# An attention block with a mixer MLP in one kernel: the last 64 rows of a product contracted beside row maxima, three maxima inside a product instead of four, and q loaded in step 2

## The chip, the core and the metric

The kernel runs on one core of one Trainium2 chip. The metric is the device time of one execution in microseconds (us): before the change the median of three runs is 1121.79 us (1120.84 to 1122.47). One further execution was taken by the profiler, and the trace is that execution's.

## The reference

Everything is float32 with S = 2048 tokens, D = 448 columns, H = 16 heads of 28 columns and an MLP of F = 1792. LN is layer norm without weights.

```python
mod = (silu(c) @ w_mod).reshape(1, 6, 1, 448)          # sa, ca, ga, sb, cb, gb
h = LN(x) * (1 + ca) + sa
q, k, v = split(h @ wqkv)                              # 16 heads of 28 columns
p = softmax(q @ k.T * 28 ** -0.5)                      # 2048 x 2048 for each head
x = x + ga * ((p @ v) @ wo)
h = LN(x) * (1 + cb) + sb
x = x + gb * (gelu(LN(h) @ w1 + b1) @ w2 + b2)
```

The softmax subtracts the maximum of each row of the scores before the exponential. The kernel has to find these row maxima before it can compute the exponentials, and most of what follows is about where it does so.

## The kernel before, in words

**Precision.** Matmuls read a rounded 32-bit form. To get float32 products, an operand is split into a rounded part `hi` and the residual `lo`, and a product is the sum of hi·hi, hi·lo and lo·hi.

**Stages.** Setup (0 to 29 us) computes the modulation of the first half and splits the weights. Stage 1 (29 to 168 us) computes q, k and v. Stage 2 (168 to 826 us) is the attention. Stage 3 (827 to 1121 us) is the MLP.

**Stage 1** runs over four blocks b of 512 tokens, and in each block over *tasks*, written (b,n) here. A task is one product with 448 contracted rows: q or k of four heads (a head group g) for 512 tokens (`qk_task`, L415), or v for 128 tokens (`v_task`, L450). In blocks 1 and 2 there are eleven tasks: q and k of the groups 1 and 2, q of group 3 (whose k is carried in spare columns of the others), four of v, and q and k of group 0 of the next block. Block 3 has eight, and the last has no maxima. 448 rows are three chunks of 128 and one of 64. `terms448` (L400) makes eleven matmuls of them, three for each full chunk and two for the last. In the last chunk x stands twice: rows 0 to 63 hold its hi part, rows 64 to 127 its residual (`split_chunk`, L280), and the weights' rows are doubled too, so that one matmul of 128 rows gives hi·hi and lo·hi together and a second gives hi·lo. `mm_acc` (L390) issues the eleven; at the middle it can call a *mid-product visit*, `emit_mid` (L715), which is set for the tasks (1,1), (1,3), (1,5), (1,7) and (2,8) only.

**Row maxima.** One maximum is a matmul (L476) that contracts the 28 columns of a head for 128 queries with 512 keys, and a reduction on VectorE (L481). The four heads of a group stand in partitions 0, 32, 64 and 96, the *row groups* 0 to 3 of TensorE; row groups 0 and 1 are called half 0, and 2 and 3 half 1. A unit (a head group g and a block qt of 512 queries) needs 64 such maxima: 4 heads, 4 tiles of queries, 4 chunks of keys. There are 16 units, so 1024 maxima. In stage 1 some are found in *pairs*: with the difference of two key chunks as operand, max(a, b) = b + relu(a − b), where ScalarE takes the relu (L489) and VectorE adds and reduces in one instruction (L493). Which units and query tiles may pair in stage 2 stands in `PAIR_ROWS` and `PAIR_AT` (L36, L37; there the relu is L641 and the reduction L648).

`emit_task` (L691) issues the maxima that follow a product: four in block 0 and five after it, a sixth in a tile of its own where `p1_n[1]` allows it, with one to three pairs (`p1_n[2]`). It takes the pairs from the front of their list, emits their difference matmuls, then two single maxima, then the second matmuls of the pairs, then the other singles. The results go through a ring of PSUM tiles (`ma`, `ma`, `m2`, `m2`, `m1` at most; in the profile `ma` and `m`), and the next matmul into a tile waits for VectorE to have read it. `p1_n` is set for each task at L837 and below.

**Stage 2** takes the 16 units one after the other, each in 16 *steps* of 128 keys (kt = 0 to 15), 256 steps in all; `clock[0]` is the step's number. A step has twelve score matmuls (L1297), six for each half, two exponentials on ScalarE (L1310) and the product with v of the step before (L1255). Beside them stand maxima of the units that come next, `n_max` of them: before step `RING` (119) four in even steps and three in odd ones (or two and the closing of a pair). `n0` of them go between the score matmuls of the first half and are sought in half 1 (`emit_single(1, ...)`); the others come at the end of the step and are sought in half 0. From `RING` on a step has one single maximum and `emit_pair` (L670): two maxima of one half in one two-bank tile, reduced together (L684); where no such couple is ready, it puts two single maxima one after the other into that tile. Steps 8 to 11 of the last four units (`is_wo`) hold the output product with `wo` and three maxima.

**What ends a unit's preparation.** When the last of a unit's 64 maxima is counted, `max_fin` reduces them, and two steps later they are written into spare rows of the unit's q tile by four DMAs (L525, L528). The q tile must have been loaded by then: `load_q` (L777, whose DMAs are at L770; `slot_b` in the profile) is asked for in step 6 of the unit before. When 64 maxima of a key chunk or of a query block are counted, the next head group's k or q for its maxima is loaded (`load_hi`, L508, `kh` and `qh` in the profile); `loaded` makes these available three steps later. All these DMAs are issued by SyncE, whose queue (SPq in the profile) works in program order: one that waits holds up those behind it. In it stand also, for the unit that has ended, the sums of the softmax (`den`, L998, step 1 of the next unit), their reciprocals to memory and back (L1006 and L1008, step 4, or step 2 in the last units), and the next group's operands (`load_k`). GpSimd multiplies by the reciprocals in step 10 (L1013), in step 7 of the last unit.

Of the kernel before, what the change touches and what calls it, by code (L numbers as in the profile page):

```python
# [16 lines left out]
ALU = mybir.AluOpType  # L17
# [5 lines left out]
D = 448  # L23
# [8 lines left out]
NTT = S // 128  # L32
P1RATE = 4
LAST_MAX = NKT - 4
RING = 119
PAIR_AT = (2, 2, 0, 2)  # L36
PAIR_ROWS = {(0, 2): 2, (0, 3): 3, (1, 0): 2, (1, 1): 2}  # L37
WO_MAX = 3
YTAGS = [f"{a}{i}" for a in ("kh", "qh") for i in range(4)]
EPS = 1e-5  # L40
# [4 lines left out]
def tile_adaln_block(ctx: ExitStack, tc: tile.TileContext, x, wqkv, wo, w1, b1, w2, b2, c, w_mod, out):  # L45
# [72 lines left out]
    def f(t):  # L118
        return t.bitcast(F32)
# [160 lines left out]
    def split_chunk(k, full, hi, lo, eng, hi_copy=None):  # L280
        if hi_copy:
            hi_copy(hi, full)
        if k < 3:
            eng.tensor_tensor(out=lo, in0=full, in1=f(hi), op=ALU.subtract)
        else:
            eng.tensor_tensor(out=hi[64:128], in0=full[64:128], in1=f(hi)[64:128], op=ALU.subtract)

    hT = {}

# [102 lines left out]
    def mm_acc(p, terms, mid=None):  # L392
        for i, (a, b) in enumerate(terms):
            if mid and i == len(terms) // 2:
                mid()
            pe.matmul(p, a, b, start=(i == 0), stop=(i == len(terms) - 1))  # L396

    def terms448(x_hi, x_lo, w_hi, w_lo):  # L400
# [13 lines left out]

    def qk_task(b, kind, g, begun=None):  # L415
        p, ts = begun or qk_terms(b, kind, g)
        if begun is None:
            mm_acc(p, ts, p1_n[3])
        emit_task(*p1_n[:3])
        if g == 0:  # L420
            tg = ("kh" if kind else "qh") + str(b)
            hi = sb.tile([128, 512], F32R, tag=tg, name=nm(tg), bufs=1)
            (kh_sb if kind else qh_sb)[(g, b)] = hi
        elif g == 1 and b < 2:

            hi = sbt("raw" if kind else "osb", [128, 512], F32R, bufs=3 if kind else 2)
            (kh_sb if kind else qh_sb)[(g, b)] = hi
        else:
            hi = sbt("hi", [128, 512], F32R, bufs=3)
        full = sbt("full", [128, 512], bufs=3)  # L430
        lo = sbt("lo", [128, 512], F32R, bufs=3)
        act.copy(full, p)

        def split():
            (act.copy if b else dve.tensor_copy)(hi, full)
            if kind == 1 and (g, b) == (0, 1):
                k_diff.append(sbt("raw", [128, 512], F32R, bufs=3))
                pool.tensor_tensor(out=k_diff[0], in0=f(hi), in1=f(kh_sb[(0, 0)]), op=ALU.subtract)
            pool.tensor_tensor(out=lo, in0=full, in1=f(hi), op=ALU.subtract)
            sl = slice(b * 512, (b + 1) * 512)  # L440
            for part, t in enumerate((hi, lo)):
                sp.dma_start(f(dscr[kind][part][g])[:, sl], f(t))

            if b < 3 or g == 0 or (kind, g) == (0, 1):
                put_spare()
            spare.append((kind, g, sl))

        return split

    def v_task(b, t, p):  # L450
        ts = slice(t * 128, (t + 1) * 128)
        hh, hl = hT[b]
        mm_acc(p[:, :D], terms448(
            lambda k: hh(k)[:, ts], lambda k: hl(k)[:, ts], lambda k: wv[0][:, k, :], lambda k: wv[1][:, k, :],
        ), p1_n[3] if phase1[0] else None)
        if phase1[0]:
            emit_task(*p1_n[:3])
        act.copy(v_sb[b][:, t, :, :DH], p[:, :D].rearrange("p (h d) -> p h d", d=DH))


# [2 lines left out]
    mxq = []  # L463
# [224 lines left out]
            emit_single(half, lambda: t[:, jj])  # L688


    def emit_task(n, sixth, n_pairs):  # L691
        if not n:
            return
        pairs = [pxq.pop(0) for _ in range(min(n_pairs, len(pxq)))]
        rests = [pair_diff(*m) for m in pairs]
        js = [m[3] for m in pairs]
        n_ops = n - len(pairs) + (sixth and len(pairs) > 0)
        singles = []
        for x in range(n_ops - len(pairs)):
            if mxq:  # L700

                free = [j for j in range(4) if j not in js] or range(4)
                fits = [y for y, m in enumerate(mxq[:16]) if m[:3] == mxq[0][:3] and m[4] == free[x % len(free)]]
                singles.append(mxq.pop(fits[0] if fits else 0))
        ops = [lambda ps, m=m: max_one(*m, ps) for m in singles]
        ops[2:2] = rests
        for x, op in enumerate(ops):
            op(ps_o if x + len(pairs) == 5 else ps_mx)
        for g, qt, cch, i, j in singles:
            count(g, qt, [cch])  # L710
        for g, qt, i, j in pairs:
            count(g, qt, [0, 1])


    def emit_mid():  # L715
        for j in range(4):
            fits = [x for x, m in enumerate(mxq[:16]) if m[4] == j]
            if fits:
                m = mxq.pop(fits[0])
                max_one(*m)  # L720
                count(*m[:2], [m[2]])

    p1_n = [0, False, 1, None]

    def finish_max(g, qt):
        if px_open and px_open[0][0][:2] == (g, qt):
# [86 lines left out]
    for b in range(NB):  # L813
# [12 lines left out]
        for n, (tb, kind, g) in enumerate(tasks):  # L826
            post = []
            ready, newq = newq, []
            if not more and n == len(tasks) - 2:

                mx_ring[:] = ["ma", "ma", "m2", "m2", "m1"]
            p1_n[0] = P1RATE if b < 1 else P1RATE + 1
            if not more and n == len(tasks) - 1:
                p1_n[0] = 0

            k = n - (6, 4, 4, 4)[b]
            p1_n[1] = not (more and (0 <= k < NC)) and not (b == 1 and n < 4)  # L837
            p1_n[2] = (3 if n > 4 else 1) if b == 3 else 2 if b == 2 and p1_n[1] else 1
            p1_n[3] = emit_mid if (b, n) in ((1, 1), (1, 3), (1, 5), (1, 7), (2, 8)) else None
            if kind < 2:  # L840
                fn = qk_task(tb, kind, g, firsts[n] if b == 0 and n < 3 else None)
                if g == 0:
                    fn()
                else:
                    post.append(fn)
                if kind == 1 and (g == 0 or (g == 1 and tb < 2)):
                    newq = [(g, qt, cch) for qt in range(tb + 1) for cch in range(tb + 1) if max(qt, cch) == tb]
            else:
                v_task(tb, g, ps_s())
            for item in ready:  # L850
                queue_max(*item)
            if b == 0 and 2 <= n < 6:
                prep_w(2, n - 2, act.copy, dve)
            if more:
                k = n - (6, 4, 4, 4)[b]

                if b == 0 and n in (0, 1, 3, 4):
                    x = 2 * n if n < 2 else 2 * n - 2
                    for fn in stages[x : x + 2]:
                        fn(xs_next)  # L860
                if b and n < 4:
                    stages[n](xs_next)
                if 0 <= k < NC:
                    post.append(h_chunk(b + 1, xs_next, k))
                if later and 7 <= n < 11:
                    later[n - 7](None)
            if n == (4 if b else 6):
                v_init(b)
            if b == 0 and n == 6:
                mod_load(0)  # L870
                mod_load(1)
            if b == 1 and n == 8:
                put_last_rows()
            if b == 2 and n == 5:
                sp.dma_start(b1_col, b1.rearrange("(k p) -> p k", p=128))
            if b == 1:
                if n < 2:
                    mod_mm(n)
                    mod_load(2 + n)
                elif n in (2, 3):  # L880
                    mod_mm(n)
                    if n == 3:
                        mod_fin()
            if not more:
                if n == 0:
                    load_q(0)
                    load_q(1)
                if n == 4:
                    load_k(0, 0)
                if n == 5:  # L890
                    act.activation(cols[:, 0:1], zero_col, AF.Exp)
                if n == 2:
                    put_ones(0)
            tick_late()
            if not more and n == 5:
                for ch in range(1, 4):
                    load_k(0, ch)
            for fn in post:
                fn()
# [331 lines left out]
    def is_wo(s_):  # L1231
        return s_ // NKT >= NU - NB and 8 <= s_ % NKT < 12
# [30 lines left out]
    for u in range(NU):  # L1263
        g, qt = divmod(u, NB)
        for kt in range(NKT):
            step = u * NKT + kt
            if kt == 6 and u + 1 < NU and u + 1 not in qst:
                load_q(u + 1)
            clock[0] = step
            if kt == LAST_MAX and u + 1 < NU:  # L1270
# [11 lines left out]
            more = ring and not three and extra(step)  # L1282
            late_one, after = after, more
            n_max = 0 if ring else WO_MAX if is_wo(step) else 4 - step % 2
            n0 = 1 if step % 4 == 3 else 2
            closing = bool(px_open) and step % 2 == 1

            ks, qs = kst[(g, kt // 4)], qst[u]
# [153 lines left out]
```

## Time and profile before

| | before |
|---|---|
| median of 3 runs | 1121.79 us (1120.84 to 1122.47) |
| the profiled execution | 1122.83 us |
| its span in the trace | 1120.9 us |
| mean granted TensorE clock | 0.996 |

| stretch of the span (us) | length | PE busy | DVE busy | ACT busy |
|---|---|---|---|---|
| 28.90 to 168.18, stage 1 | 139.28 | 138.44 | 113.65 | 83.90 |
| 168.18 to 461.90, stage 2 before RING | 293.72 | 293.31 | 265.27 | 251.50 |
| 461.90 to 823.00, stage 2 from RING on | 361.10 | 355.28 | 265.78 | 283.36 |
| 827.00 to 1120.90, stage 3 | 293.90 | 289.13 | 142.72 | 57.83 |

In the quoted lines PE is TensorE with its matmuls, PEld its weight loads, DVE VectorE, ACT ScalarE, POOL GpSimd and SPq the queue of SyncE. `L396` is line 396 of the kernel. A timeline line gives the start in us, the duration from the first start to the last end of the group, the engine, line and operation, the tile written and the tiles read, and how many instructions of that kind the line stands for. In brackets stands the idle time before it and what ended it. A line of windows gives a stretch and its length, then for PE, PEld, DVE, ACT and POOL (or, where the view was asked for one engine, for those that apply) the busy time and the number of instructions, then the granted clock, the DMA share and GB/s; where the view is narrowed to one line of the kernel, the first pair is that line's matmuls and the second its weight loads.

### The profile page before, as it was taken

Reading aid. Unit: us, or ns where it says so; the run is one execution under the profiler, and the core shown is the slowest. Engines: PE = TensorE matmul, PEld = TensorE weight load, DVE = VectorE, ACT = ScalarE, POOL = GpSimd, SP = SyncE. Lnnn points to the kernel's source line nnn. Section 1 sums busy time; section 2 is a strip of 40 time slices with the busy share of each in tenths; the row PEclk is TensorE's granted clock in tenths of the full one; section 3 lists DMA queues with packets and bytes.
Section 4 is the critical chain, followed back from the end, with each engine's and each line's share of the span. In section 5 each row is a group of like instructions: output and inputs, shape, how many; then the busy total and the mean of one; then the engine's idle time right before and its main releaser. Section 6 shows DMA issues by size and latency. Waiting matters only on the chain.

```text
span 1120.9 us, 20683 instructions
## 1 busy us (share of the span) xinstructions
PE 1105.9 (99%) x8319; PEld 669.6 (60%) x8319; DVE 807.3 (72%) x1393; ACT 693.9 (62%) x878; POOL 214.9 (19%) x215
## 2 busy tenths in 40 slices
PE   9999999999999999999899999999999999999998
PEld 6756675444444444444344454545568888888887
DVE  6968788999989989988788867573648853444322
ACT  4555657888888888888788878576752311111210
POOL 2533333010000000000100020206214504023000
PEclk9999999999999999999999999999999999999999
DMA  8563263121132101231211412111322100000000
GB/s 309 200 200 93 88 201 112 31 86 33 56 114 59 57 30 58 58 87 58 76 40 39 143 30 87 57 30 58 91 69 78 31 33 1 1 33 1 33 1 33
DMA packets 49341, 81.19 MB, mean 72 GB/s; under 512 B 12311, under 2 KB 18702, under 8 KB 49234
## 3 DMA queue, kind: packets, MB, share of 16 engines
q1 hardware_dynamic: 48762, 79.14, 22.7%
q8 instruction: 65, 1.06, 0.4%
q10 hardware_dynamic: 148, 0.46, 0.1%
q0 software_dynamic: 336, 0.28, 0.1%
q14 instruction: 30, 0.25, 0.1%
HBM read 55.04 MB, written 26.48 MB: 73 GB/s over the span
## 4 chain that ended last, share of the span: by engine, by line
PE 92%; DVE 3%; DMA 2%; ACT 1%; issue 1%; SPq 0%; POOL 0%; DVEq 0%; ACTq 0%; POOLq 0%
PE s L1297 22%; PE o L1255 22%; PE m L396 16%; PE pa L396 8%; PE m L476 8%; PE s L1377 3%; PE s L1378 3%; PE s L1376 3%; DVE mxp L481 2%; PE s L476 2%; PE t L1377 1%; PE t L1378 1%; PE t L1376 1%; PE ma L476 1%; DMA slot_c<-in_w_mod_dram 1%
## 5 line engine op out<-in xcount | busy, mean ns | idle before, releaser
L481 DVE TENSOR_REDUCE mxp<-m 128x1 f32<-128x512 f32 x564 | 365.8, 686 | 87.4 <-PE m L476 68.6
L1297 PE MATMUL s<-slot_b,slot_a 28*128 28x512 f32 (+1 forms) x3072 | 360.0, 425 | 0.5 <-ACT slot_c0h L1310 0.5
L1297 PEld LDWEIGHTS s<-slot_b,slot_a 28*128 28x128 f32 (+1 forms) x3072 | 212.6, 184 | 172.5 <-ACT slot_c L1310 91.4
L476 PE MATMUL m<-kh,qh 28*128 28x512 f32 x598 | 222.0, 469 | 4.2 <-DMA kh<-d 3.3
L1310 ACT ACTIVATE slot_c<-s 128x1024 f32<-128x1024 f32 x170 | 174.8, 1028 | 57.8 <-PE s L1297 56.2
L1255 PE MATMUL o<-slot_c,v 128*32 128x512 f32 x680 | 179.6, 607 | 0.0
L1353 ACT ACTIVATE full<-m,b_col 128x512 f32<-128x512 f32 x56 | 38.6, 689 | 191.9 <-PE m L396 179.7
L1255 PE MATMUL o<-slot_c1h,v 128*32 128x512 f32 x512 | 136.3, 611 | 0.9 <-ACT slot_c1h L1310 0.9
L1255 PE MATMUL o<-slot_c0h,v 128*32 128x512 f32 x512 | 134.7, 605 | 0.0
L1310 ACT ACTIVATE slot_c0h<-s 128x1024 f32<-128x1024 f32 x128 | 131.4, 1026 | 3.4 <-PE m L396 2.4
L684 DVE TENSOR_REDUCE mxp<-s 128x2 f32<-128x1024 f32 x104 | 127.5, 1226 | 5.1 <-PE s L476 0.6
L1310 ACT ACTIVATE slot_c1h<-s 128x1024 f32<-128x1024 f32 x128 | 130.7, 1021 | 0.0
L1356 DVE CAST hi<-full 128x512 fp32r<-128x512 f32 x56 | 25.2, 450 | 135.1 <-ACT full L1353 135.1
L1310 ACT ACTIVATE slot_d<-s 128x1024 f32<-128x1024 f32 x86 | 88.3, 1027 | 29.1 <-PE s L1297 26.3
L476 PEld LDWEIGHTS m<-kh,qh 28*128 28x128 f32 x598 | 89.8, 182 | 20.6 <-DVE mxp L481 12.3
L1255 PE MATMUL o<-slot_d,v 128*32 128x512 f32 x344 | 91.4, 610 | 0.4 <-ACT osb L1219 0.4
L1013 POOL TENSOR_TENSOR osb<-osb,osb 128x512 f32<-128x512 f32 x16 | 20.9, 1306 | 365.7 <-DMA osb<-drec 306.0
L396 PE MATMUL m<-y,slot_a 128*128 128x512 f32 x160 | 60.7, 395 | 0.0
L648 DVE CUSTOM_DVE_ANT_0 slot_d0i<-m,slot_d0i 128x512 f32<-128x512 f32 x55 | 38.0, 691 | 15.2 <-PE m L476 12.8
L476 PE MATMUL s<-kh,qh 28*128 28x512 f32 x210 | 47.7, 441 | 0.8 <-DVE mxp L481 0.8
L1357 DVE TENSOR_TENSOR lo<-full,hi 128x512 fp32r<-128x512 f32 x56 | 44.1, 788 | 5.2
L1255 PEld LDWEIGHTS o<-slot_c,v 128*32 128x32 f32 x680 | 24.5, 108 | 39.0 <-issue 36.5
(342 smaller groups left out, 1845.6 us busy)
## 6 DMA issues: line engine op xcount, KB each, us to landing
slot_b<-d SPq DMA_DIRECT2D x32, 256.0 KB
slot_a<-d SPq DMA_DIRECT2D x32, 256.0 KB
d<-lo SPq DMA_DIRECT2D x28, 256.0 KB
d<-hi SPq DMA_DIRECT2D x16, 256.0 KB
osb<-drec SPq DMA_DIRECT2D x15, 256.0 KB
out_dram<-xn SPq DMA_DIRECT2D x16, 224.0 KB
raw<-in_B_w_dram SPq DMA_DIRECT2D x14, 224.0 KB
qh<-d SPq DMA_DIRECT2D x12, 256.0 KB
```

Of the source, the lines that this page charges most:

```text
L396: pe.matmul(p, a, b, start=(i == 0), stop=(i == len(terms) - 1))
L476: pe.matmul(m, qh_sb[(g, qt)][js, i * 128 : (i + 1) * 128], k[js, :], start=True, stop=True)
L481: dve.tensor_reduce(out=mxp[(g, qt)][:, i, j, cch : cch + 1], in_=m, op=ALU.max, axis=AX.X)
L684: dve.tensor_reduce(out=mxp[(g, qt)][:, i, j : j + 2, cch], in_=t, op=ALU.max, axis=AX.X)
L1255: pe.matmul(o[32 * j : 32 * j + 32, :], v_sb[kt // 4][:, kt % 4, 4 * g + j, :], p[j // 2][:, j % 2, :], start=(kt == 0), stop=(kt == NKT - 1),
L1297: pe.matmul(s2[:, jj, :], ks[rows_, kp, kc], qs[rows_, qp, :], start=(term == 0), stop=(term == 2))
L1310: act.activation(pt[hf], s2, AF.Exp, scale=SCALE)
L1353: act.activation(gf, p, AF.Gelu_apprx_tanh, bias=b1_col[:, i : i + 1])
L1357: dve.tensor_tensor(out=glo, in0=gf, in1=f(ghi), op=ALU.subtract)
L1376: pe.matmul(pp, ghi[:, ts], w_hi, start=(m == 0), stop=False)
L1377: pe.matmul(pp, ghi[:, ts], w_lo, start=False, stop=False)
L1378: pe.matmul(pp, glo[:, ts], w_hi, start=False, stop=(m == NFT - 1))
```

## The change

Five edits are made together.

1. **The last 64 rows beside maxima.** x's chunk of 64 rows now holds its residual in rows 0 to 63 and its hi part in rows 64 to 127. A new function `mm_beside` issues ten of a product's eleven matmuls in full; the eleventh, x's hi part by the weights' residual, is issued on rows 64 to 127 alone, inside `emit_task`, behind the pairs' second matmuls. It is used in blocks 2 and 3 wherever maxima follow, and in (1,8), (1,9) and (1,10): 21 tasks. (The residual of x times the residual of the weights, which the full matmul had added, falls away there.)
2. **`emit_task`** now chooses the pairs so that their row groups differ, those of half 0 first where a 64-row matmul stands beside them, else those of half 1; it looks among the first 32 single maxima for wanted row groups; and it emits first as many singles as make four with the pairs, then the pairs' second matmuls, the 64-row matmul, and the remaining singles.
3. **`emit_mid`** issues three maxima instead of four, starting at a row group that rotates.
4. **`load_q`** is called in step 2 of the unit before instead of step 6.
5. **Constants of stage 2.** `RING` is 121 instead of 119; `PAIR_ROWS` has an entry more, which allows unit (1,2) three of its four query tiles for pairs instead of four; `n0` is 1 in every fourth step only if that step is not one of those with `wo`, so that those have two maxima first and one after them.

```diff
-RING = 119
+RING = 121
-PAIR_ROWS = {(0, 2): 2, (0, 3): 3, (1, 0): 2, (1, 1): 2}
+PAIR_ROWS = {(0, 2): 2, (0, 3): 3, (1, 0): 2, (1, 1): 2, (1, 2): 3}
...
-            eng.tensor_tensor(out=hi[64:128], in0=full[64:128], in1=f(hi)[64:128], op=ALU.subtract)
+            eng.tensor_tensor(out=hi[0:64], in0=full[0:64], in1=f(hi)[0:64], op=ALU.subtract)
...
+    def mm_beside(p, terms):
+        for i, (a, b) in enumerate(terms[:-2] + terms[-1:]):
+            if p1_n[3] and i == len(terms) // 2:
+                p1_n[3]()
+            pe.matmul(p, a, b, start=(i == 0), stop=False)
+        a, b = terms[-2]
+        emit_task(*p1_n[:3], lambda: pe.matmul(p, a[64:128], b[64:128], start=False, stop=True))
...
-        if begun is None:
-            mm_acc(p, ts, p1_n[3])
-        emit_task(*p1_n[:3])
+        if begun is None and p1_n[4]:
+            mm_beside(p, ts)
+        else:
+            if begun is None:
+                mm_acc(p, ts, p1_n[3])
+            emit_task(*p1_n[:3])
...
-    def emit_task(n, sixth, n_pairs):
+    def emit_task(n, sixth, n_pairs, beside=None):
...
-        pairs = [pxq.pop(0) for _ in range(min(n_pairs, len(pxq)))]
+        pairs = []
+        for _ in range(min(n_pairs, len(pxq))):
+            taken = [m[3] for m in pairs]
+            pairs.append(min(pxq, key=lambda m: (m[3] in taken, (m[3] < 2) != (beside is not None))))
+            pxq.remove(pairs[-1])
...
+        want = [j for j in (2, 3, 0, 1) if j not in js] + [j for j in (0, 1) if j not in js] + [0, 1]
...
-                free = [j for j in range(4) if j not in js] or range(4)
-                fits = [y for y, m in enumerate(mxq[:16]) if m[:3] == mxq[0][:3] and m[4] == free[x % len(free)]]
-                singles.append(mxq.pop(fits[0] if fits else 0))
+                near = [m for m in mxq[:32] if m[:2] == mxq[0][:2]]
+                singles.append(min(near, key=lambda m: m[4] != want[x]))
+                mxq.remove(singles[-1])
+        first = max(0, 4 - len(pairs))
...
-        ops[2:2] = rests
-        for x, op in enumerate(ops):
-            op(ps_o if x + len(pairs) == 5 else ps_mx)
+        ops[first:first] = rests + ([beside] if beside else [])
+        done = len(pairs)
+        for op in ops:
+            if op is beside:
+                beside()
+            else:
+                op(ps_o if done == 5 else ps_mx)
+                done += 1
...
     def emit_mid():
-        for j in range(4):
-            fits = [x for x, m in enumerate(mxq[:16]) if m[4] == j]
+        base = len(mxq)
+        for j in range(3):
+            fits = [x for x, m in enumerate(mxq[:16]) if m[4] == (base + j) % 4]
...
+            p1_n[4] = b > 1 and p1_n[0] > 0 or (b, n) in ((1, 8), (1, 9), (1, 10))
...
-            if kt == 6 and u + 1 < NU and u + 1 not in qst:
+            if kt == 2 and u + 1 < NU and u + 1 not in qst:
                 load_q(u + 1)
...
-            n0 = 1 if step % 4 == 3 else 2
+            n0 = 1 if step % 4 == 3 and not is_wo(step) else 2
```

More of the change, by code (lines that the diff above doesn't have):

```diff
@@ L452, in v_task @@
         hh, hl = hT[b]
-        mm_acc(p[:, :D], terms448(
+        terms = terms448(
             lambda k: hh(k)[:, ts], lambda k: hl(k)[:, ts], lambda k: wv[0][:, k, :], lambda k: wv[1][:, k, :],
-        ), p1_n[3] if phase1[0] else None)
-        if phase1[0]:
-            emit_task(*p1_n[:3])
+        )
+        if phase1[0] and p1_n[4]:
+            mm_beside(p[:, :D], terms)
+        else:
+            mm_acc(p[:, :D], terms, p1_n[3] if phase1[0] else None)
+            if phase1[0]:
+                emit_task(*p1_n[:3])
         act.copy(v_sb[b][:, t, :, :DH], p[:, :D].rearrange("p (h d) -> p h d", d=DH))
@@ L700, in emit_task @@
             if mxq:
-                free = [j for j in range(4) if j not in js] or range(4)
-                fits = [y for y, m in enumerate(mxq[:16]) if m[:3] == mxq[0][:3] and m[4] == free[x % len(free)]]
-                singles.append(mxq.pop(fits[0] if fits else 0))
+                near = [m for m in mxq[:32] if m[:2] == mxq[0][:2]]
+                singles.append(min(near, key=lambda m: m[4] != want[x]))
+                mxq.remove(singles[-1])
+        first = max(0, 4 - len(pairs))
         ops = [lambda ps, m=m: max_one(*m, ps) for m in singles]
-        ops[2:2] = rests
-        for x, op in enumerate(ops):
-            op(ps_o if x + len(pairs) == 5 else ps_mx)
+        ops[first:first] = rests + ([beside] if beside else [])
[3 more added lines that the diff above has]
+                beside()
+            else:
+                op(ps_o if done == 5 else ps_mx)
+                done += 1
         for g, qt, cch, i, j in singles:
@@ L721, in emit_mid @@
                 count(*m[:2], [m[2]])
-    p1_n = [0, False, 1, None]
+    p1_n = [0, False, 1, None, False]
     def finish_max(g, qt):
```

## The prediction

> **What bounds the kernel now.** I read the busy shares of the page first, then the chain that ended last.
>
> ```profile
> PE 1105.9 (99%) x8319; PEld 669.6 (60%) x8319; DVE 807.3 (72%) x1393; ACT 693.9 (62%) x878; POOL 214.9 (19%) x215
> PE 92%; DVE 3%; DMA 2%; ACT 1%; issue 1%; SPq 0%; POOL 0%; DVEq 0%; ACTq 0%; POOLq 0%
> ```
>
> TensorE is the bound throughout, so a microsecond is gained only where TensorE has less to do one after the other, or where it stands still. Such places have to be looked for in the timeline. One task of stage 1 on TensorE (window 138 to 146; start, duration, count):
>
> ```profile
> 138.41 1.19 PE L396 MATMUL pa<-slot_c,slot_a 128*128 128x512 f32 x4
> ...
> 140.80 0.39 PE L396 MATMUL pa<-slot_c0h,slot_a2h 128*128 128x512 f32 x1
> 141.12 0.50 PE L476 MATMUL m<-raw,qh 28*128 28x512 f32 x2
> 141.12 0.49 PE L476 MATMUL m<-raw,osb 28*128 28x512 f32 x1
> 141.46 0.39 PE L476 MATMUL o<-kh,qh 28*128 28x512 f32 x1
> 141.46 0.40 PE L476 MATMUL ma<-raw,osb 28*128 28x512 f32 x1
> 141.70 0.39 PE L476 MATMUL ma<-kh,qh 28*128 28x512 f32 x1
> 142.02 1.19 PE L396 MATMUL pa<-slot_c,slot_a 128*128 128x512 f32 x4
> ...
> 144.19 0.61 PE L396 MATMUL pa<-slot_c0h,slot_a 128*128 128x512 f32 x2
> 144.74 0.49 PE L476 MATMUL m<-raw,qh 28*128 28x512 f32 x1
> ...
> 145.07 0.39 PE L476 MATMUL ma<-kh,qh 28*128 28x512 f32 x2
> 145.40 0.97 PE L396 MATMUL pa<-slot_c,slot_a 128*128 128x512 f32 x3
> ```
>
> The ten starts from 138.41 to 140.80 lie 2.39 us apart in steps of about 0.23: that is what one product matmul costs (its 0.39 is latency). Matmuls of 28 rows in different row groups start together (141.12, three). Six maxima take 0.66 us in two rounds (144.74 to 145.40) and 0.90 in three (141.12 to 142.02), where two of them wanted the same row group. A change from 128 rows to 28 costs about 0.09 beyond the 0.23 (140.80 to 141.12 is 0.32).
>
> **A. Three mid-product maxima instead of four.** Task (1,5) before, on TensorE and then on VectorE:
>
> ```profile
> 78.78 0.73 PE L476 MATMUL m<-raw,osb 28*128 28x512 f32 x2
> 79.44 0.47 PE L396 MATMUL pa<-slot_e,slot_c0h 128*128 128x448 f32 x1
> ...
> 80.86 0.50 PE L476 MATMUL m<-raw,qh 28*128 28x512 f32 x1
> 80.87 0.49 PE L476 MATMUL ma<-raw,osb 28*128 28x512 f32 x2
> 81.41 0.50 PE L476 MATMUL m<-kh,qh 28*128 28x512 f32 x1
> 82.01 0.49 PE L476 MATMUL m<-raw,osb 28*128 28x512 f32 x1
> 82.43 0.66 PE L277 MATMUL o<-ident,xn 128*128 128x128 f32 x4
> ```
>
> ```profile
> 79.48 1.28 DVE L481 TENSOR_REDUCE mxp<-ma 128x1 f32<-128x512 f32 x2
> 80.68 1.28 DVE L481 TENSOR_REDUCE mxp<-m 128x1 f32<-128x512 f32 x2
> 81.87 1.27 DVE L481 TENSOR_REDUCE mxp<-ma 128x1 f32<-128x512 f32 x2
> ```
>
> The group at the end takes 1.57 us (80.86 to 82.43) instead of 0.66, because nine results in one task go through five PSUM tiles and VectorE frees one only every 0.60 us (80.68, then 81.87: two apart). One visit fewer takes one reduction, 0.60, out of that wait; five tasks have such a visit: 3.0 us. In the middle, four visits took a second round here (78.78 to 79.44 is 0.66); three in three row groups need one of 0.43 (0.66 less the 0.23). I count that in three of the five tasks: 0.7. **A = −3.7.** The five maxima do not vanish; they move to stage 2 and are paid for under D.
>
> **B. Sixty-four rows beside maxima.** 21 tasks have it: three with b=1, eleven with b=2, seven with b=3. The full product loses one matmul of 0.23; a matmul on rows 64 to 127 comes back behind the first round. The trace holds no matmul of 64 rows beside one of 28. Its nearest rows disagree. Rows of 28 in disjoint groups share their time fully (144.74 above), which makes the new matmul free beside maxima of groups 0 and 1. Against it speaks the one place where 64 rows follow 28:
>
> ```profile
> 72.47 0.50 PE L476 MATMUL m<-raw,osb 28*128 28x512 f32 x1
> 72.90 0.96 PE L747 MATMUL o<-slot_v,slot_d 64*32 64x448 f32 x8
> ```
>
> A lone maximum of row group 3 (that it is group 3 follows from the order that L691 to L710 write out) and then modulation matmuls whose first uses rows 0 to 63: they start 0.43 later, so they waited for it to drain, although the rows are disjoint. But these are also only 32 columns wide, where maxima and the new matmul have 128. The cost is between 0 and 0.43 for a separate turn, and another turn where a maximum still follows. I take 0, as the row that shares the new matmul's width has it, and keep the other end as a rival.
>
> Not all 21 gain. Pairs of row groups 0 and 1 are 24 in all; counted off task by task they run out in tasks (2,8) to (2,10), are not there yet in (3,0), and (3,5) and (3,6) take a third pair from group 2 or 3: there the new matmul meets its own row groups and gets a round to itself, no gain. In (1,8) to (1,10) VectorE is full:
>
> ```profile
> 94.69:105.60 10.91, 10.91 (x53) 7.38 (x51) 10.84 (x23) 4.69 (x9) 2.72 (x3) 1.00 0.31 95
> ```
>
> (10.84 of 10.91 us, the fourth number). That leaves 12 tasks at 0.23: 2.8 us. The new choice of row groups also ends third rounds like the one at 141.70; three of the tasks have one, 0.24 each: 0.7. **B = −3.5.** What is late next is VectorE: in the (3,n) tasks five reductions at 0.60 are 3.0 us against a new period of 3.15, so it just fits.
>
> **C. q asked for in step 2.** The SyncE queue and TensorE in steps 145 to 155:
>
> ```profile
> 529.39 0.59 SPq L998 DMA_DIRECT2D den<-osb  x1
> ...
> 537.82 0.32 SPq L1006 DMA_DIRECT2D drec<-den  x1
> ...
> 539.83 0.95 SPq L770 DMA_DIRECT2D slot_b<-d  x2
> 545.74 2.28 SPq L528 DMA_DIRECT2D slot_b<-full  x4
> 548.07 0.91 SPq L508 DMA_DIRECT2D kh<-d  x2
> ```
>
> ```profile
> 552.20 0.46 PE L476 MATMUL m<-kh,qh 28*128 28x512 f32 x1 [3.26 <-DMA kh<-d]
> ```
>
> ```profile
> 178.44:461.93 283.49, 172.57 (x1357) 101.55 (x1358) 1.00 0.19 55
> 474.30:537.13 62.83, 36.85 (x338) 22.34 (x338) 1.00 0.24 69
> ```
>
> ```profile
> 548.44:557.96 9.52, 6.26 (x50) 2.46 (x47) 3.95 (x6) 3.85 (x5) 0.00 (x0) 0.82 0.27 84
> ```
>
> Issued at 539.83, q has to land before its maxima may be written into it (L528, 545.74), and the k that was asked for in step 150 waits behind these four until 548.07. TensorE stands until 552.20 and then runs at a lower clock (0.82 in that stretch). At 12 score matmuls a step the two windows between hold 113 steps of 2.51 us (before RING) and 28 of 2.24 (after); steps 154 and 155 took 9.52 where 4.49 is usual: 5.0 us lost. With the load in step 2 of the same unit, behind nothing but den<-osb, it is out some four steps earlier, about 530 (den left at 529.4); with the same 5.9 us to land and 2.3 for the four the queue is free by 538.3, and kh leaves some ten microseconds ahead of 548. What it is moved past: drec and osb<-drec of the same unit now stand behind it, but drec waits for VectorE's reciprocal (it left at 537.8 before), and GpSimd multiplies osb only in step 10 of the unit, by the times in the code. kh or qh loads asked for in steps 2 to 5 are now the ones held back, up to two steps, inside the three that `loaded` grants. **C = −5.0.**
>
> **D. Later constants.** Five steps at the end of stage 2 that have no maxima:
>
> ```profile
> 771.86:781.77 9.91, 9.91 (x101) 3.79 (x101) 3.85 (x10) 9.22 (x11) 8.06 (x7) 1.00 0.43 149
> ```
>
> RING 121 makes two steps 2.51 instead of 2.24: +0.5. By count (119 steps before cover 472 maxima, 121 after cover 478, with one pair more by RING and two fewer by PAIR_ROWS) 342 are left at RING instead of 343, so the last one falls in step 234 instead of 233: +0.3, the price of a step with maxima (2.24) over one without (1.98). **D = +0.8.** The order two and one in step 203 and its like moves one matmul inside a step: 0. One more place stands open, step 230:
>
> ```profile
> 745.62 0.40 PE L476 MATMUL s<-kh,qh 28*128 28x512 f32 x1
> 746.80 0.49 PE L476 MATMUL s<-kh,qh 28*128 28x512 f32 x1 [0.78 <-DVE mxp L481]
> ```
>
> ```profile
> 744.65:752.38 7.73, 6.95 (x50) 2.98 (x46) 3.99 (x6) 3.97 (x5) 1.26 (x1) 0.78 0.06 20
> ```
>
> No pair of row groups 0 and 1 was left, so L684's fallback put two single maxima one after the other into one tile, and two steps took 7.73 instead of 4.49: 3.2 us, the low clock included. The last maxima fall otherwise after the change; I count 0, with −3.2 (gone) and +3.2 (one more) as ends.
>
> **The sum**: −3.7 −3.5 −5.0 +0.8 = −11.4 us. The profiled execution took 1122.8 (span 1120.9 and 1.9 around it), 1.0 over the median of 1121.8; against the median the forecast is **1110.4**.
>
> **Rivals.** *Drain.* If a change between 28 and 64 rows empties the array, the new matmul takes 0.43 by itself, less the 0.23: +0.20 in 13 tasks, and another 0.43 in the eight in which a maximum follows it: 7.6 us, of which I take 1 to hide behind VectorE in (1,8) to (1,10) and (2,8). Less the 0.7 of the rounds B is then +5.9 and the sum −2.0: **1119.8**. The rows at 72.47 speak for it, those at 144.74 neither way. The Trainium skill says it outright: TensorEngine Tiling, Key Properties, has it that changing the tiling mode, and not just the tile, drains TensorE; by that rule the time is this rival's, and the rows at 72.47 agree with it (0.43). The Trainium skill's page TensorE: Matmul & The Clock Gate, Part 3, The mechanism, lets a weight load overlap whenever the row groups differ, which would give 1110.4; no row here shows 64 rows beside 28 at one width.
>
> *The queue stays in the way.* Another k load falls into steps 2 to 5 of a unit and stalls as at 548: C is 0, **1115.4**. Against it: on my count the g=3 loads come in steps 148 to 155, the held-back ones in 146 to 149.
>
> *One half runs dry* (the other side). B takes its pairs from row groups 0 and 1, so stage 1 leaves more work in groups 2 and 3, by my tally about 20 maxima, where before RING the surplus was 17 and gave one fallback. Each fallback costs 3.2 us. If the pairs of half 0 end before step 222 instead of 230, five are added: 1110.4 + 16 = **1126.4**; together with the drain two are enough. From four on the gain of 11.4 is eaten.
>
> **Chances.** Forecast 0.48, spread 1105 to 1113.5 by the end of step 230 and by A (0.60 to 0.85 a task); drain 0.22 (1116 to 1121); queue 0.11; half runs dry, alone or with the drain, 0.19. A measurement of this kernel tells about 0.2%, 2.2 us, from no change. Faster: 0.48 + 0.11 + half of the drain = 0.70; same, the other half, 0.11; slower 0.19. The range runs from 1105 to 1121, which leaves out the dry half and the best end of the forecast.
>
> **What would show it.** A: the end group of (1,5) near 0.9 us instead of 1.57. B: in (2,1) to (2,7) ten starts, then maxima and the 64-row matmul starting with the second round, 0.66 together; under the drain it starts 0.4 behind it. C: slot_b<-d issued some ten microseconds before step 150, no wait on kh<-d. D: 121 long steps, and whether a pair of single maxima stands in one tile near step 230. The prediction is wrong if the periods of (2,1) to (2,7) do not fall by 0.23, or if a new wait over 1 us stands in stage 2.

## The result, and the profile after

The change makes the kernel a little faster: the median of 20 runs is 1119.99 us (1119.19 to 1121.06) against 1122.03 us of 20 runs of the kernel before, a ratio of 0.9981 with a 95% interval of 0.9974 to 0.9987. That is 2 us, where 11.4 were forecast. The time lies at the forecast's rival "drain" (1119.8). The profiled execution took 1120.38 us.

The first page of the profile after, with the lines that answer to the two that opened the prediction:

```profile
PE 1108.2 (99%) x8319; PEld 668.7 (60%) x8319; DVE 808.3 (72%) x1394; ACT 694.8 (62%) x877; POOL 215.4 (19%) x215
PE 95%; DVE 2%; ACT 1%; issue 1%; DMA 0%; POOL 0%; ACTq 0%; DVEq 0%; POOLq 0%
```

DMA has left the chain, TensorE's share of it has grown from 92 to 95%, and TensorE is busy 2.3 us longer than before with the same number of matmuls. So waits went, and something on TensorE got dearer. The windows of the two stages tell where, before and then after (the span's time from the first row maximum to the first score matmul is stage 1, and from there to the MLP stage 2):

```profile
28.90:168.18 139.28, 138.44 (x709) 94.67 (x709) 113.65 (x238) 83.90 (x153) 55.36 (x57) 1.00 0.48 156
168.18:826.93 658.75, 651.66 (x6143) 307.34 (x6142) 531.05 (x843) 537.74 (x604) 90.51 (x92) 0.99 0.22 65
```

```profile
29.73:173.30 143.57, 143.30 (x704) 94.66 (x703) 111.22 (x233) 85.61 (x153) 55.44 (x57) 1.00 0.47 153
173.30:824.32 651.02, 648.02 (x6148) 305.91 (x6148) 534.47 (x849) 536.91 (x603) 90.93 (x92) 1.00 0.22 66
```

Stage 1, which was to get 7.2 us shorter, is 4.3 longer, with five maxima fewer. Stage 2 is 7.7 shorter. Setup ends 0.8 later; in the nine profiles of this study with the same setup it ends anywhere between 28.9 and 30.3, so this is not the change's.

Task (3,2) after, on TensorE (L490 is a maximum's matmul, L402 one of the ten full ones, L404 the one of 64 rows):

```profile
154.80 0.50 PE L490 MATMUL m<-raw,qh 28*128 28x512 f32 x1
...
154.81 0.72 PE L490 MATMUL ma<-kh,qh 28*128 28x512 f32 x2
155.46 0.49 PE L404 MATMUL pa<-slot_c0h,slot_a 64*128 64x512 f32 x1
155.88 0.50 PE L490 MATMUL o<-kh,qh 28*128 28x512 f32 x1
156.31 0.50 PE L402 MATMUL pa<-slot_c,slot_a 128*128 128x512 f32 x1
```

The two rounds of maxima take 0.66 as ever (154.80 to 155.46). The 64-row matmul does not start with the second round but after it, and for 0.42 no other matmul starts, though by the code the one maximum of the second round stands in row group 1. The maximum behind it, in a tile that is free, takes another 0.43. What was to save 0.23 costs 0.85 here, less the 0.23 of the matmul that fell away from the product.

The task with a visit of three, (1,5), stands so:

```profile
78.89 0.50 PE L490 MATMUL m<-raw,osb 28*128 28x512 f32 x2
79.32 0.47 PE L396 MATMUL pa<-slot_e,slot_c0h 128*128 128x448 f32 x1
...
80.75 0.63 PE L490 MATMUL m<-raw,osb 28*128 28x512 f32 x3
81.49 0.50 PE L490 MATMUL ma<-kh,qh 28*128 28x512 f32 x1
81.91 0.66 PE L277 MATMUL o<-ident,xn 128*128 128x128 f32 x4
```

One round in the middle, 0.43 instead of 0.66, and 1.17 at the end (to 81.91, from a first maximum at 80.74) instead of 1.57, where about 0.9 was forecast. The end of this task still waits for VectorE once (80.75, then 81.49).

Steps 145 to 151 in SyncE's queue (L795 is the load of q, L542 the writes of maxima into it, L522 a load of k or q for maxima):

```profile
534.95 0.58 SPq L1024 DMA_DIRECT2D den<-osb  x1
535.65 0.88 SPq L795 DMA_DIRECT2D slot_b<-d  x2
538.97 2.60 SPq L542 DMA_DIRECT2D slot_b<-full  x4
541.68 0.45 SPq L522 DMA_DIRECT2D kh<-d  x1
543.19 0.32 SPq L1032 DMA_DIRECT2D drec<-den  x1
...
548.49 0.32 SPq L522 DMA_DIRECT2D kh<-d  x1
```

The load of q now comes right behind den<-osb and ahead of drec, the four writes are through at 541.6, and `osb<-drec` behind them at 545.8. The next k load leaves at 548.49, in step 151, with nothing ahead of it in the queue, right behind the last maximum that reads its tile (which ends at 548.46). The windows of steps 154 and 155 and of steps 230 and 231:

```profile
553.95:558.40 4.45, 4.45 (x51) 1.90 (x47) 3.72 (x5) 3.90 (x5) 0.00 (x0) 1.00 0.00 0
745.12:749.55 4.43, 4.43 (x52) 1.91 (x48) 3.81 (x5) 3.73 (x5) 1.28 (x1) 1.00 0.03 10
```

9.52 us became 4.45, and 7.73 became 4.43: no stall, no fallback, and the clock at 1.00 in both.

### The profile page after: what moved, and what is told of

It is laid out like the page before. It is cut to its first block, busy times and chain, and to the rows that moved or that the text cites. A ratio compares the mean times of both kernels' runs of the same rounds, so it can differ in the third digit from the quotient of the medians.

```text
span 1118.3 us, 20712 instructions
## 1 busy us (share of the span) xinstructions
PE 1108.2 (99%) x8319; PEld 668.7 (60%) x8319; DVE 808.3 (72%) x1394; ACT 694.8 (62%) x877; POOL 215.4 (19%) x215
## 4 chain that ended last, share of the span: by engine, by line
PE 95%; DVE 2%; ACT 1%; issue 1%; DMA 0%; POOL 0%; ACTq 0%; DVEq 0%; POOLq 0%
PE s L1323 22%; PE o L1281 22%; PE m L396 16%; PE m L490 8%; PE pa L402 4%; PE pa L396 4%; PE s L1403 3%; PE s L1402 3%; PE s L1404 3%; PE s L490 2%; PE t L1403 1%; PE t L1404 1%; PE t L1402 1%; DVE mxp L495 1%; PE pa L404 1%
## 5 line engine op out<-in xcount | busy, mean ns | idle before, releaser
L495 DVE TENSOR_REDUCE mxp<-m 128x1 f32<-128x512 f32 x570 | 369.7, 686 | 84.2 <-PE m L490 72.6
L490 PE MATMUL m<-kh,qh 28*128 28x512 f32 x608 | 225.6, 469 | 0.9 <-ACT full L1070 0.4
L490 PEld LDWEIGHTS m<-kh,qh 28*128 28x128 f32 x608 | 91.1, 182 | 17.6 <-DVE mxp L495 12.7
L662 DVE CUSTOM_DVE_ANT_0 slot_d0i<-m,slot_d0i 128x512 f32<-128x512 f32 x54 | 37.3, 691 | 14.6 <-PE m L490 11.4
L490 PE MATMUL s<-kh,qh 28*128 28x512 f32 x206 | 45.8, 440 | 0.0
```

The costliest lines, as they stand in the source:

```text
L490: pe.matmul(m, qh_sb[(g, qt)][js, i * 128 : (i + 1) * 128], k[js, :], start=True, stop=True)
L495: dve.tensor_reduce(out=mxp[(g, qt)][:, i, j, cch : cch + 1], in_=m, op=ALU.max, axis=AX.X)
```

## The experiments

The theory after the result: a change of the contracted rows between 28 and 64 takes TensorE a turn of its own, about 0.42 us, and this turns B from a gain into a loss of some 6 us; A, C and D did about what was forecast. The rival: the 64-row matmul costs nothing, and stage 1 grew because the maxima are chosen and ordered in another way, or because PSUM tiles come free late.

### The whole product again

```diff
     def mm_beside(p, terms):
-        for i, (a, b) in enumerate(terms[:-2] + terms[-1:]):
...
-        emit_task(*p1_n[:3], lambda: pe.matmul(p, a[64:128], b[64:128], start=False, stop=True))
+        mm_acc(p, terms, p1_n[3])
+        emit_task(*p1_n[:3], lambda: None)
```

> The changed kernel with all eleven matmuls of a product in full and no 64-row matmul among the maxima; the choice and the order of the maxima, and everything else, are the changed kernel's. Theory one (a change of the contracted rows between 28 and 64 takes a turn of its own, about 0.42 us, and a second one where a maximum follows): 13 tasks give back 0.2 us and eight give back 0.4 to 0.6, 6 us in all less about 1 where VectorE is full, so about 1114.5 us (1113.5 to 1116). Theory two (the 64-row matmul costs nothing, and stage 1 grew because of the new choice and order of the maxima or of PSUM tiles that come free late): 21 matmuls of 0.23 come on top, 1120 to 1125.

Measured: 1113.65 us (1113.33 to 1114.42), a ratio to before of 0.9917 (0.9903 to 0.9932). Stage 1, and stage 2 for comparison:

```profile
29.12:166.43 137.31, 137.05 (x704) 94.70 (x704) 110.87 (x233) 83.97 (x153) 55.35 (x57) 1.00 0.49 158
166.43:817.41 650.98, 648.03 (x6149) 306.03 (x6148) 534.42 (x849) 536.92 (x603) 91.08 (x92) 1.00 0.22 66
```

Stage 2 is that of the changed kernel to 0.04 us, and stage 1 is 6.26 us shorter. So the 64-row matmul in place of a full one costs 6.3 us over 21 tasks, and without it the other edits make the kernel over 8 us faster than before. That is also faster than both kernels.

### The 64-row matmul behind all maxima

```diff
-        ops[first:first] = rests + ([beside] if beside else [])
+        ops[first:first] = rests
+        if beside:
+            ops.append(beside)
```

> The changed kernel with the 64-row matmul behind all maxima of its task instead of ahead of the last one in the eight tasks that have one there. Theory one (a turn of 0.42 us at each change of the contracted rows): the eight tasks lose one change, 0.42 each, but the maximum that follows may need a third round of 0.23 in some, so 1.5 to 3.4 us are gained, 1116.6 to 1118.5. Theory two (no turn of its own): 1120.0 within 0.5.

Measured: 1117.21 us (1116.88 to 1117.71), ratio 0.9948 (0.9934 to 0.9963). Task (3,2):

```profile
152.39 0.49 PE L490 MATMUL m<-raw,qh 28*128 28x512 f32 x1
...
152.74 0.39 PE L490 MATMUL o<-kh,qh 28*128 28x512 f32 x1
153.05 0.50 PE L404 MATMUL pa<-slot_c0h,slot_a 64*128 64x512 f32 x1
153.48 1.20 PE L402 MATMUL pa<-slot_c,slot_a 128*128 128x512 f32 x4
```

The maximum in o now runs in the second round (152.74), and one of the two turns is gone, as theory one has it. The other stays: 153.05 to 153.48 is 0.43, so the last position is still worse than a full matmul in the product (stage 1 is 140.50 long, against 137.31 with the whole product).

### The turn by itself

Two kernels append sequences of matmuls behind the last product. The first has eight rows of them, in most of which a couple is repeated eight times. One of the rows, 28 with 64:

```diff
+    for _ in range(8):
+        pe.matmul(bank[0], w_[0:28, :128], w_[0:28, :], start=True, stop=True)
+        pe.matmul(bank[1], w_[64:128, :128], w_[64:128, :], start=True, stop=True)
```

> The changed kernel with eight rows of matmuls of 128 columns by 512 behind the last product of the MLP, results unused: 128 rows eight times, and then, eight times each, 28 rows at 0 with 28 at 64, 28 at 0 with 64 at 64, 28 at 0 with 32 at 64, 64 at 0 with 64 at 64, 128 with 64, 128 with 28, and two of 28 with two of 64. Theory one (a turn of its own at each change of the contracted rows between 28 or 32, 64 and 128): couples of 28 with 28, 28 with 32 and 64 with 64 take 0.23 us each, the mixed ones 0.7 to 0.85. Theory two (only shared row groups make a matmul wait): 28 with 64 takes 0.23 like 28 with 28, and 128 with anything 0.46. The time of the kernel grows by the sum of these, 25 to 40 us, and says nothing else.

It took 1177.61 us in its one execution, 57 more than the profiled one of the changed kernel, where 25 to 40 were expected. The granted clock fell to 0.50 in the third row and later again:

```profile
1118.44:1119.83 1.39, 1.39 (x15) 1.00 0.00 0
1120.80:1123.35 2.55, 2.55 (x8) 1.00 0.03 6
1124.49:1128.09 3.60, 3.60 (x6) 0.50 0.00 0
```

The first column is the window, then its length, TensorE's busy time with its matmuls and the clock. Six couples of 28 with 28 took 1.39, 0.23 a couple. In 28 with 64, six starts lie in 2.55, 0.43 each, and 0.72 each at the lower clock. Since the row of 28 with 32 fell wholly into the lower clock, it was taken again in a second kernel, with 32 full matmuls ahead of each sequence of four couples. The first of its five sequences:

```diff
+    for _ in range(32):
+        pe.matmul(bank[0], w_[:, :128], w_, start=True, stop=True)
+    for _ in range(4):
+        pe.matmul(bank[0], w_[0:28, :128], w_[0:28, :], start=True, stop=True)
+        pe.matmul(bank[1], w_[64:96, :128], w_[64:96, :], start=True, stop=True)
```

> The changed kernel with five short sequences of matmuls behind the last product of the MLP, results unused, each behind 32 matmuls of 128 rows so that the granted clock has time to return: four times 28 rows at 0 with 32 at 64, 28 at 0 with 64 at 64, 64 at 0 with 64 at 64, 128 with 28 at 64, and 128 with 64 at 64. If a change of the contracted rows between 32 (or 28), 64 and 128 takes a turn of its own whatever the granted clock: at clock 1.00 the couples 28 with 32 and 64 with 64 take 0.23 us, and each matmul of the mixed couples starts 0.43 behind the one before. Rival (28 and 32 rows count as different too, or the low clock made the couples what they were): 28 with 32 also 0.43 each, or 64 with 64 not 0.23.

One execution, at a clock of 1.00 throughout. Rows of 28 with 32, of 28 with 64, of 64 with 64, and of 128 with 64:

```profile
1123.29 0.39 PE L1440 MATMUL m<-hi 28*128 28x512 f32 x1
1123.29 0.39 PE L1441 MATMUL o<-hi 32*128 32x512 f32 x1
1123.53 0.39 PE L1440 MATMUL m<-hi 28*128 28x512 f32 x1
...
1132.41 0.50 PE L1445 MATMUL m<-hi 28*128 28x512 f32 x1
1132.84 0.50 PE L1446 MATMUL o<-hi 64*128 64x512 f32 x1
...
1142.83 0.39 PE L1450 MATMUL m<-hi 64*128 64x512 f32 x1
1142.84 0.39 PE L1451 MATMUL o<-hi 64*128 64x512 f32 x1
1143.07 0.39 PE L1450 MATMUL m<-hi 64*128 64x512 f32 x1
...
1162.45 0.50 PE L1460 MATMUL m<-hi 128*128 128x512 f32 x1
1162.89 0.50 PE L1461 MATMUL o<-hi 64*128 64x512 f32 x1
```

28 with 32 and 64 with 64 start together, 0.23 a couple (1123.29 to 1123.53; 1142.83 to 1143.07). 28 and 64, in disjoint row groups and both 128 columns wide, start 0.43 apart, and so do 128 and 64, and 128 and 28 (five starts from 1152.20 to 1153.91 and on to 1154.33). Theory one holds and the rival falls: not the row groups but the height of the tile (the contracted rows) decides, 32 (28 counts as this), 64 or 128. The weight loads tell why it is 0.43 and not 0.23: in the first of the two kernels, at clock 1.00, one starts only when its matmul does:

```profile
1123.35 0.18 PEld L1443 LDWEIGHTS m<-hi 28*128 28x128 f32 x1 [0.25 <-issue]
1123.35 0.50 PE L1443 MATMUL m<-hi 28*128 28x512 f32 x1
```

0.18 for the weights and then 0.25 for the rows. In one height the load lies under the matmul before: in the couples of 64 with 64 one stands at 1142.83, where the couple before starts, for the couple at 1143.07. The Trainium skill's rule (TensorEngine Tiling, Key Properties) that a change of the tiling mode drains TensorE agrees with these rows.

### The choice of the maxima

From the run with the whole product, `emit_task` is set back to its old choice and order:

```diff
-            pairs.append(min(pxq, key=lambda m: (m[3] in taken, (m[3] < 2) != (beside is not None))))
...
+        pairs = [pxq.pop(0) for _ in range(min(n_pairs, len(pxq)))]
...
+        ops[2:2] = rests
```

> The run with the whole product (eleven full matmuls, the rest as in the changed kernel), and with the choice and order of pairs and single maxima in stage 1 as they were before the change. Theory one (the new choice makes third rounds of 0.23 in some tasks): stage 1 gets 0.5 to 1.0 us shorter; what stage 2 does with the other remainder is open by one fallback of 3.2. Rival (the new choice ends third rounds, as the prediction had it): stage 1 gets 0.7 longer.

Measured: 1112.64 us (1112.33 to 1113.44), ratio 0.9911 (0.989 to 0.9933), the fastest of the study. Its stage 1:

```profile
29.12:165.48 136.36, 136.10 (x704) 93.89 (x704) 110.90 (x233) 83.81 (x153) 55.21 (x57) 1.00 0.49 159
```

0.95 shorter than with the new choice (137.31). In task (2,6) of the changed kernel one sees where:

```profile
126.81 0.50 PE L490 MATMUL m<-raw,qh 28*128 28x512 f32 x1
...
127.15 0.39 PE L490 MATMUL m<-kh,qh 28*128 28x512 f32 x1
...
127.39 0.39 PE L490 MATMUL m<-kh,qh 28*128 28x512 f32 x1
```

Three rounds (126.81, 127.15, 127.39) where the kernel before had two (125.58 and 125.92, 0.66 in all). The 64-row matmul has no part in this: with the whole product the task has the same three rounds.

### Four visits again

```diff
-        for j in range(3):
+        for j in range(4):
```

> The run with the whole product, with four maxima in the five mid-product visits again. Theory one (stage 1 pays 0.4 for the fourth at the end of the task and 0.25 for its second round): stage 1 gets 2.5 to 3.0 us longer, and stage 2 has five maxima less, 0.3 to 1.5 shorter: 1.5 to 2.5 us above the run with the whole product. Rival (VectorE is not what the end of those tasks waits for): within 1 us of it.

Measured: 1119.29 us (1118.34 to 1120.48), ratio 0.9975 (0.9963 to 0.9987), 5.6 above the run with the whole product. Stage 1 is 139.87, 2.56 longer, as theory one said. But stage 2 got no shorter; it took 653.87, 2.9 more. In one step of it, number 142, the fallback is back (2.2 us are usual there), with the clock at 1.00:

```profile
523.73:527.42 3.69, 2.91 (x27) 1.23 (x24) 2.36 (x4) 2.55 (x3) 0.00 (x0) 1.00 0.28 71
```

So the expectation was right on stage 1 and missed 3 us in stage 2: 1.5 of them are this fallback (TensorE waits 0.78 for VectorE to have read the tile), 0.8 more lie in step 152, where TensorE waits 0.49 for a k load, and the rest is spread over steps, at most 0.3 in each. Fewer maxima for stage 2 to find did not make it shorter.

### q in step 2 alone, and q in step 6 again

The kernel before with the one line changed:

```diff
-            if kt == 6 and u + 1 < NU and u + 1 not in qst:
+            if kt == 2 and u + 1 < NU and u + 1 not in qst:
```

> The kernel before with one edit: q asked for in step 2 of the unit before. Theory one (the k load of step 150 was held up behind writes that waited for q): the stall of steps 154 and 155 goes and nothing else changes, 5.0 us less than before, a ratio of 0.9955. Rival (another wait takes its place, or the stall belongs to something else): within 0.2% of before.

Measured: 1116.31 us (1116.02 to 1118.29), ratio 0.9947 (0.9927 to 0.9967). Steps 230 and 231, then 154 and 155:

```profile
739.56:745.72 6.16, 5.38 (x50) 2.34 (x47) 3.99 (x6) 3.98 (x5) 1.26 (x1) 1.00 0.02 7
548.37:552.92 4.55, 4.55 (x50) 1.96 (x47) 4.15 (x6) 3.99 (x5) 0.00 (x0) 1.00 0.39 115
```

The 9.52 are 4.55, 5.0 us as forecast. The fallback of step 230 is still there, with the same wait of 0.78 us, but costs 1.7 and not 3.2: half of that price was the lower clock of the kernel before in this place.

The clock has a part in the 5.0 as well. In the profiled execution of the kernel before it stood at 0.50 for 3.41 us from 553.08 on, and again from 747.64 on; 3.26 us of waiting and half of 3.41 make the 5.0. Other executions of the same kernel do not pay this: of the 40 that ran beside the experiments three show a mean clock of 1.000 and took 1118.6, 1119.0 and 1120.3 us, about as long as the changed kernel, and the eight at 0.993 to 0.995 took 1123.2 to 1126.6. The price of a stall is thus its wait, and in most executions of this kernel, not in all, a stretch at the lower clock behind it.

The reverse, the changed kernel with the line set back:

> The changed kernel with q asked for in step 6 of the unit before again. Theory one (the earlier q cleared SyncE's queue before the k load of step 150): the stall near step 154 is back, 4 to 5 us, 1124 to 1125.5. Theory two (the stall went because the maxima end in other steps now, whatever q does): within 0.5 of the changed kernel's 1120.0.

Measured: 1125.39 us (1121.82 to 1126.98), ratio 1.0018 (1.0007 to 1.0029), 5.4 above the changed kernel. The size is theory one's, but the place is not: steps 154 and 155 are undisturbed, and the stall stands in steps 25 and 26, with the same order in SyncE's queue (L542 the writes into q, L522 the k):

```profile
230.44 2.21 SPq L795 DMA_DIRECT2D slot_b<-d  x2
235.96 2.27 SPq L542 DMA_DIRECT2D slot_b<-full  x4
238.27 0.44 SPq L522 DMA_DIRECT2D kh<-d  x1
```

```profile
237.88:248.18 10.30, 8.01 (x53) 3.14 (x50) 5.16 (x9) 4.72 (x6) 0.00 (x0) 0.67 0.10 26
```

```profile
241.44 0.79 PE L490 MATMUL m<-kh,qh 28*128 28x512 f32 x2 [2.29 <-DMA kh<-d]
```

q asked for in step 22 leaves at 230.44, the writes wait for it until 235.96, and the k behind them until 238.27; its maximum starts at 241.44. The two kernels differ in this one line and, beyond 0.3 us in a step, in the time of these two steps alone, so the queue is the cause. Which unit it strikes hangs, by the code, on the step in which the last maximum of a key chunk falls.

### The old constants

From the run with the whole product:

```diff
-RING = 121
+RING = 119
...
-PAIR_ROWS = {(0, 2): 2, (0, 3): 3, (1, 0): 2, (1, 1): 2, (1, 2): 3}
+PAIR_ROWS = {(0, 2): 2, (0, 3): 3, (1, 0): 2, (1, 1): 2}
...
-            n0 = 1 if step % 4 == 3 and not is_wo(step) else 2
+            n0 = 1 if step % 4 == 3 else 2
```

> The run with the whole product, with RING 119, the entry for unit (1,2) out of PAIR_ROWS, and the steps with wo in their old order. Theory one (the later RING costs 0.5 to 0.8 and it is the constants that keep a couple of half 0 for step 230): 0.7 less for two long steps and one fallback of 3.2 more, about 2.5 us above the run with the whole product. Rival (the fallback went because stage 1 leaves other maxima, not by the constants): 0.7 below it.

Measured: 1118.53 us (1116.52 to 1120.94), ratio 0.9965 (0.9952 to 0.9979), 4.9 above the run with the whole product. Neither expectation had the place: step 230 is as short as with the new constants, and two other places stall, step 72 and steps 88 and 89:

```profile
350.69:355.07 4.38, 2.82 (x29) 1.20 (x25) 2.74 (x6) 2.67 (x4) 1.28 (x1) 1.00 0.11 39
392.82:400.74 7.92, 6.82 (x53) 2.87 (x50) 4.73 (x9) 4.82 (x6) 1.28 (x1) 0.78 0.09 31
```

```profile
347.87 0.43 SPq L518 DMA_DIRECT2D qh<-d  x1
```

In the first TensorE waited 1.6 us, from 351.4 to 352.98. The profile puts this down to the clearing of a unit's maxima on VectorE, but that was over at 352.06; the q for the maxima, which left SyncE's queue only at 347.87, landed at 352.89 by its signals in the trace, and this is what ended the wait. In the second it waited 1.1 us for a k that left at 388.14, after which the clock was lower. Both loads left right behind `osb<-drec` (347.22 and 387.54). By the code a load can be used from the third step after it was asked for, so these two were asked for by steps 69 and 85, step 5 of their units, and came late by way of the queue: it is what the rival "the queue stays in the way" described, though not in the changed kernel. The later end of the maxima eats what RING gives: stage 2 behind step 118 is not shorter with the old constants. What each of the three constants does alone was not tried.

## Why the prediction was wrong, point by point

**B is the step that failed**: "I take 0, as the row that shares the new matmul's width has it, and keep the other end as a rival." The other row was the right one. The wait at 72.47, 0.43, is the price that a change of height has in the two kernels of matmuls at 128 columns, so the 32 columns, which I took as an excuse for it, are not needed to explain it. Against the whole product the 64-row matmul measures +6.26 where −2.8 was forecast; the rival "drain" had 6.6 for it (its 7.6 less the 1 behind VectorE). The rows at 144.74, which I followed, are all of one height and could not tell. The sign named for it came out against it: the period from the maxima of (2,1) to those of (2,2) was to fall by 0.23 from 3.44, and is 3.61. The second part of B failed as well: the new choice was to end third rounds (−0.7), and with it there are four that the kernel before has not, in (1,4), (2,5), (2,6) and (3,0), while the one at 141.70 is still there; against the old choice stage 1 is 0.95 longer. B is +7.2 instead of −3.5.

**A** was right in mechanism and a little too large: stage 1 with three visits and the old choice is 2.92 shorter than before (139.28 to 136.36), against 3.7. The end of a task gives back 0.4 on the mean of the five and not 0.6 (0.63 in (1,3), 0.10 in (1,7)): in (1,5), as shown, VectorE still holds up one matmul. The second round in the middle is gone in three tasks, 0.24 or 0.26 each, as counted.

**C** was right: 5.0 us, shown by itself, and in the reverse by the stall that comes back in another unit. Some 1.7 of the 5.0 are the lower clock behind the wait (3.41 us at 0.50).

**D** measures +1.0 against +0.8. The two steps 119 and 120 took 4.43 before and 5.17 after, 0.74 more, and step 234, with the last maxima, 4.80 instead of 4.53. What the prediction did not see is that the constants also keep loads from coming late: put back alone they cost 4.9 us, most of it in steps 72, 88 and 89. D counted them as a price alone.

**Step 230** was counted at 0 with −3.2 as its lower end, and came out at that end: 7.73 to 4.43. Nothing in the prediction worked this out, so it is luck. The fallback there is also gone with the old choice, with the old constants and with four visits (4.44, 4.44 and 4.43 for the two steps), and stays with q alone; which edit moved it is not shown.

The sum of what was measured in the spans: −2.9 (A) +7.2 (B) −5.0 (C) +1.0 (D) −3.3 (step 230) is −3.0, with the later setup (+0.8) −2.2; the spans differ by 2.6, and the other 0.4 lies in small differences of steps. The rival "drain" hit the time to 0.2 us, but in part by chance: it had B at 5.9 rather than 7.2 and A 0.8 too large, and it had no gain at step 230. The rivals "queue stays in the way" and "one half runs dry" did not come in the changed kernel: it shows no wait over 1 us in stage 2.

## What to carry to other kernels

A matmul that is short in contracted rows runs beside others only if they have the same tile height; beside others, count it as a turn with its weight load in the open (0.43 instead of 0.23 here), and a second one if the old height comes back behind it. Where two rows of a trace disagree on an operation that it does not show, the row with the same change in it weighs more than the row with the same shape. And a stall of a queue that works in program order is to be taken away at its cause: with q late, edits that moved the maxima only moved the stall, from step 154 to step 25, and even with q early two other loads came late, in steps 72 and 88, under constants that look unrelated.

## What the hardware showed beside this

The granted clock fell to 0.50 while single tiles of 28 and 64 rows took turns (from 1123.8 in the first of the two sequences of matmuls), though TensorE was never idle from 1116.09 on. With 32 full matmuls ahead of each short sequence it stayed at 1.00; a wait of 1.20 us stands ahead of the first matmul in both kernels. Whether the turns caused the lower clock was not tried. At 0.50 a turn of its own costs 0.72 and not 0.43.
